# A front of one batch with its divisions split over two engines, its casts moved, its fillers changed and one weight loaded in whole rows

## The chip, the cores and the metric

The kernel runs on one core of one Trainium2 chip. The core has a matrix engine (TensorE, PE in the profile), three engines for elementwise work (VectorE or DVE, ScalarE or ACT, GpSimd or POOL), a queue engine that only issues transfers (SyncE, SP), and 16 DMA engines that all queues share. The metric is the device time of one execution in microseconds, as a median over several runs; lower is better.

## The reference

A linear attention with cosine weights is followed by an MLP mixer. There are 8 batches, 8 heads, 576 positions and 64 channels per head; the result x of the attention has 512 channels.

```python
r = np.maximum(x, 0.0)                       # for q and for k
phi = np.concatenate([r * cos_w, r * sin_w], axis=-1)
kv = np.einsum('bhsf,bhsd->bhfd', k_p, v);  z = np.sum(k_p, axis=2)
num = np.einsum('bhsf,bhfd->bhsd', q_p, kv)
den = np.einsum('bhsf,bhf->bhs', q_p, z)[..., None] + 1e-06
x = num / den                                # heads side by side: (8, 576, 512)
h = np.maximum(xt @ w_tok1, 0.0) @ w_tok2    # xt: x with positions last; 576 -> 256 -> 576
u = x + h.transpose(0, 2, 1)
out = u + np.maximum(u @ w_ch1, 0.0) @ w_ch2 # 512 -> 1536 -> 512
```

Inputs and output are float32; the matmuls of the kernel run in bf16.

## The kernel before

**Tiling.** The 576 positions of a batch are four chunks of 128 (position p * 4 + r is row p of chunk r) and a tail of 64. Tails of two batches share one tile, one in each half of the partitions. The chunks are taken in the order 0, 1, 2, tail, 3 (`ORDER`, line 55).

**Two kinds of work.** A `Front` (lines 217 to 545) makes x and u of a batch: features of q and k (`feature`, line 249), v cast to bf16 (`values`), key sums (`ksum`), the kv matrices (`kv`, `kv_out`), transposes of q's features (`q_trans`), the products `num_half`, the division `x_out` (line 375), the token mixing `tok1` and `tok2`. A `Channel` (lines 550 to 654) makes the two channel matmuls of a batch: `c_main` or `c_block` with w_ch1, ScalarE's ReLU into h1T, `o_step` with w_ch2, and the sum with u and the store.

**What sets the order.** The kernel has a manual schedule: each engine runs its instructions in the order in which the Python code makes them. For batches 1 to 7 a hand-made list (`pieces`, line 473) puts the parts of the next batch's front between the channel steps of the batch before. The first batch has no such cover. Its front is written out in `first_front` (line 656); there TensorE also runs `busy` matmuls (line 203), fillers on zeros that no one reads: 12 at the start, one after each group of q transposes, two for each chunk of k, one and four more later on.

**The end of the first front.** After the kv matrices have been copied out, `cast_tok1` (line 207, ScalarE, twice) casts w_tok1 to bf16. `permute_tok2` (line 210) casts w_tok2 and reorders its columns, one half on ScalarE and one on GpSimd, two instructions each. Then the chunks run in a small pipeline: `num_half` writes one half of the heads (four) into a PSUM tile `num_ps` of two banks, one bank a half; `x_out` multiplies by the reciprocal of the denominator on VectorE, with one instruction for all 8 heads, except that the first chunk goes half by half; `tok1` multiplies the result by w_tok1 into two accumulators. There are two tiles for `num_ps`, so num of a chunk waits until x of the chunk two before has been read out. After the last chunk come `tok1_out` (ReLU into B1), `turned_x` and `turned_b` (u transposed, straight from matmuls), and `c_block` (line 570): for each of the four 128-row blocks of w_ch1 (kb), the first three column blocks of the channel matmul.

**Loads.** SP issues nearly all loads, in program order. At the start come q, k and v of batch 0 in halves, then w_tok1 and w_tok2. w_ch1 is cast to bf16 by its transfer, so GpSimd issues it: four transfers of 128 x 2 x 768, two for the left half of the columns and two for the right (lines 187 to 193); the first waits for the first half of v. `load_batch(1, "kvq")` (line 776) waits for the second of them (`w_ch1_done[1]`), and SP's queue behind it waits too. Later batches' loads stand in the main loop (lines 799 to 811), which for batch 2 loads the tails of both batches of the pair in one go.

Of the kernel before, what the change touches and what calls it, by code (L numbers as in the profile page):

```python
# [9 lines left out]
F32 = mybir.dt.float32  # L10
# [6 lines left out]
def kernel(  # L17
# [15 lines left out]
    nc = tc.nc  # L33
# [149 lines left out]
        nc.gpsimd.memset(t[half(1)], 0.0)  # L183
    for g in range(2):
        nc.gpsimd.dma_start(out=w_tail1[half(g), :], in_=moe_w_tok1[SM:S, :])
    C2 = D_ch // 2
    w_ch1_done = []
    for c2 in range(2):
        for ki in range(0, NCC, 2):
            w_ch1_done.append(nc.gpsimd.dma_start(  # L190
                out=w_ch1[:, ki:ki + 2, c2 * C2:(c2 + 1) * C2],
                in_=moe_w_ch1[ki * P:(ki + 2) * P, c2 * C2:(c2 + 1) * C2]
                .rearrange("(n c) d -> c n d", c=P)))
    after(w_ch1_done[0], v_done)
    w_ch2_done = []
    def load_w_ch2(lo, hi):
# [6 lines left out]
    def busy(dst, times):  # L203
        for _i in range(times):
            nc.tensor.matmul(dst, ident, zeros[:, 0:dst.shape[-1]], start=True, stop=True)

    def cast_tok1(mi):
        nc.scalar.copy(w_tok1[:, :, mi * P:(mi + 1) * P], w_tok1n[:, :, mi * P:(mi + 1) * P])
# [8 lines left out]
    class Front:  # L217
        def __init__(self, b, res, tail):
            self.qt, self.vt, self.kt = io_tiles[b]
            self.va, self.xt = v_augs[b % 2], x_tails[b % 2]  # L220
            self.res, self.tail = res, tail
            self.rows = half(b % 2)

            self.order = ORDER if b != 2 else (*range(R), R)


            self.alone = b < 2
            self.kp, self.qp, self.d_sb = {}, {}, {}

            self.qpT = once.tile([P, R * H, P], BF16, name="qpT")  # L230
            self.kv_sb = [twos.tile([P, HH, DP], BF16, name=f"kv_sb{g}") for g in range(2)]
            self.x = once.tile([P, R, Dm], BF16, name="x_sb")
# [142 lines left out]
        def x_out(self, num_ps, ci, den=None, halves=(0, 2)):  # L375
            lo, hi = halves
            rows = self.rows_of(ci)
            if den is None:
                den = self.d_sb[ci][rows].rearrange("p (g j) o -> p g j o", g=2)
            nv = num_ps[rows, lo:hi, 0:HH * DP].rearrange("p g (j d) -> p g j d", d=DP)  # L380
            nc.vector.tensor_mul(  # L381
                self.x_of(ci)[rows].rearrange("p (g j d) -> p g j d", g=2, j=HH)[:, lo:hi],
                nv[:, :, :, 0:D],
                den[:, lo:hi].to_broadcast([rows.stop - rows.start, hi - lo, HH, D]))

        def tok1(self, mi, chunks):
            if not hasattr(self, "B1"):
# [268 lines left out]
    def first_front(f):  # L656


        idle_ps = ps_at.tile([P, 2, 512], F32, name="idle_ps", tag="at")[:, 0, :]
        lo_heads, hi_heads = (0, HH), (HH, H)  # L660
        busy(idle_ps, 12)

        for j in range(2):
            f.feature("q", 3, j, lo_heads, on_act=True)
        for heads in (lo_heads, hi_heads):
            for ci in range(R):
                if (heads, ci) != (lo_heads, 3):
                    f.feature("q", ci, 0, heads)
                    f.feature("q", ci, 1, heads)
                f.q_trans(ci, heads)  # L670
                busy(idle_ps, 1)
        f.q_side(R)
        f.q_trans(R, pool=ps_at)
        busy(idle_ps, 2)
        for ci in range(R):
            f.feature("k", ci, 0)
            f.feature("k", ci, 1, on_act=(ci > 1))
            busy(idle_ps, 2)
            f.ksum(ci)
        f.k_side(R)  # L680
        f.values(R, nc.vector)
        for ci in range(R):
            f.values(ci, nc.vector, hi_heads)
        for ci in range(R - 1):
            f.values(ci, nc.scalar, lo_heads)
        f.kv(0, (0,))
        busy(idle_ps, 1)
        f.ksum(R)
        f.ksum_out()
        f.values(R - 1, nc.scalar, lo_heads)  # L690
        f.kv(1, (0,))
        f.kv(2, (0,))
        dens = f.dens(ORDER[:2])
        f.dens_out(*dens)
        f.kv(3, (0,))
        f.kv(R, (0,))
        f.kv_out((0,))
        for ci in range(NSC):
            f.kv(ci, (1,))
        f.kv_out((1,), on_act=(1,))  # L700
        for ci in range(NT):
            cast_tok1(ci)
        permute_tok2(0, nc.scalar.copy)
        permute_tok2(1, nc.gpsimd.tensor_copy)
        f.new_uT()
        t_ps = {}

        def num(ci, fill=0):
            num_ps = ps_at.tile([P, 2, 512], F32, name="num_ps", tag="at")
            for g in range(2):  # L710
                f.num_half(num_ps, ci, g)
            busy(num_ps[:, 1, HH * DP:512], fill)
            f.x_out(num_ps, ci)

        num_ps = ps_at.tile([P, 2, 512], F32, name="num_ps", tag="at")
        f.num_half(num_ps, ORDER[0], 0)
        f.x_out(num_ps, ORDER[0], halves=(0, 1))
        dens = f.dens(ORDER[2:])
        f.dens_out(*dens)
        f.num_half(num_ps, ORDER[0], 1)  # L720
        f.x_out(num_ps, ORDER[0], halves=(1, 2))
        num(ORDER[1], fill=4)
        for i, ci in enumerate(ORDER):
            if i + 2 < NSC:
                num(ORDER[i + 2])
            for mi in range(NT):
                f.tok1(mi, (ci,))
            if i == 2:

                for kb in range(2):  # L730
                    t_ps[kb] = ps_mm.tile([P, SM], F32, name="t_ps", tag="mm")
                    f.turned_x(t_ps[kb], kb, ORDER[:2])
        for cols in (slice(0, DH), slice(DH, Dm)):
            for mi in range(NT):
                f.tok1_out(mi, on_act=(mi == 0), cols=cols)
        for kb in range(NCC):
            if kb < 2:
                f.turned_x(t_ps[kb], kb, range(2, R))
                continue
            t_ps[kb] = ps_at.tile([P, 2, 512], F32, name="t_ps", tag="at")[:, 0, :]  # L740
            f.turned_x(t_ps[kb], kb)

        c = Channel(0, f.res, f.tail)
        by_block = f.res["uT"].rearrange("p (r k) t -> p r k t", r=R)
        for kb in range(NCC):
            f.turned_b(t_ps[kb], kb, slice(0, SM))
            (nc.vector.tensor_copy if kb % 2 else nc.scalar.copy)(
                by_block[:, :, kb, :], t_ps[kb].rearrange("p (r t) -> p r t", r=R))
        for kb in range(NCC):
            for mi in range(AHEAD):  # L750
                c.c_block(mi, kb)
        return c

    def load_batch(b, which="kvq", behind=None, main=True, tails=True):
        if b not in io_tiles:
            io_tiles[b] = tiles()
        if b // 2 not in io_tails:
            io_tails[b // 2] = tail_tiles()
        qt, vt, kt = io_tiles[b]
        qtt, vtt, ktt = io_tails[b // 2]  # L760
        done = []
        for n in which:
            dst, tail_dst, src = {"k": (kt, ktt, k), "v": (vt, vtt, v), "q": (qt, qtt, q)}[n]
            if main:
                done.append(load_main(dst, src, b))
            if behind is not None and len(done) == 1:
                after(done[0], behind)
            if tails and b % 2 == 0:
                load_tail(tail_dst, src, b)
            if tails and (b % 2 == 0 or b == 1):  # L770
                load_tail(tail_dst, src, b | 1)
        return done

# [14 lines left out]
    for b in range(B):  # L788
# [4 lines left out]
        for i, step in enumerate(steps):  # L793
            step()
            for what, args in slots.pop(i, ()):
                what(*args)


            if b == 0 and i == NCH:
                load_batch(2, "kq", behind=w_ch2_done[2], tails=False)  # L800
            if b == 0 and i == NCH + 13:
                load_batch(2, "v")
                load_batch(2, "k", main=False)
            if b == 1 and i == 1:
                load_batch(2, "q", main=False)
            if b == 1 and i == 9:
                load_batch(3, "kvq")
            if 1 < b < B - 2 and i == NSC:
                load_batch(b + 2, "vq")
            if 0 < b < B - 3 and i == NCH + 12:  # L810
                load_batch(b + 3, "k")
            if i == len(steps) - 4 and b + 2 < B:
                following = next_front(b + 2)
            for what, args in following.pop(i - len(steps), ()):
                what(*args)
# [34 lines left out]
```

## Time and profile before

| | us |
|---|---|
| median of 3 runs (268.06 to 269.16) | 268.06 |
| the profiled execution, whole | 268.94 |
| its span, first to last instruction | 267.2 |
| TensorE busy in the span | 260.2 (97%) |
| VectorE busy | 165.8 (62%) |
| ScalarE busy | 127.8 (48%) |
| GpSimd busy | 14.1 (5%) |
| first matmul of a filler, first q transpose | 1.37, 6.05 |
| first `c_block` matmul (L574) | 23.58 |

How to read it: a page of the profile gives the busy time of each engine over the span, its share in 40 slices, the DMA queues, the chain of work that ended last, and the costliest groups of instructions. The timeline shows single instructions or merged runs of equal ones: start in us from the span's start, length, engine, source line, operation, output and inputs, the count, and in brackets how long the engine had stood idle just before and what ended that. A busy TensorE isn't TensorE at its peak, since matmuls overlap: a 512-wide bf16 matmul is shown with 0.38 us, while its successor starts 0.22 us after it.

### The profile page before, as it was taken

The numbers are of one execution on the slowest core, as the hardware profiler recorded it, in microseconds if no ns is written. First come the engines' busy times: TensorE is split into PE (matmuls) and PEld (weight loads), VectorE is DVE, ScalarE is ACT, GpSimd is POOL, SyncE is SP. The second block draws the span as 40 slices with busy tenths as digits, with TensorE's granted clock in tenths as the row PEclk, the third lists the DMA queues.
The fourth block names the chain that finished last, engine by engine and source line by source line (L and its number), as shares of the span: only waits on it lengthen the run. The fifth ranks groups of instructions, "written<-read, shape, count | busy, mean of one in ns | idle before, by whom it ended". The sixth has DMA issues, their size and how long they took to land.

```text
span 267.2 us, 5140 instructions
## 1 busy us (share of the span) xinstructions
PE 260.2 (97%) x2042; PEld 139.6 (52%) x2063; DVE 165.8 (62%) x381; ACT 127.8 (48%) x227; POOL 14.1 (5%) x29
## 2 busy tenths in 40 slices
PE   7999999999999999999999999999999999999995
PEld 2575465465644455446644455446644455445544
DVE  6983978785565846876565846876565846720022
ACT  4963794428506462546515362546506362516400
POOL 6060050010000000000000000000000000000000
PEclk9999999999999999999999999999999999999999
DMA  7999999879999999489854999179964570180032
GB/s 219 314 290 259 305 210 205 304 180 288 188 310 306 279 192 324 146 212 262 234 201 118 294 219 349 61 187 237 248 245 118 157 120 0 51 207 1 2 94 102
DMA packets 91079, 53.68 MB, mean 201 GB/s; under 512 B 59440, under 2 KB 85552, under 8 KB 91056
## 3 DMA queue, kind: packets, MB, share of 16 engines
q1 hardware_dynamic: 88288, 49.10, 69.5%
q0 software_dynamic: 2240, 3.74, 7.5%
q10 hardware_dynamic: 528, 0.52, 0.6%
q8 instruction: 16, 0.26, 0.4%
q14 instruction: 7, 0.06, 0.1%
HBM read 35.85 MB, written 9.44 MB: 169 GB/s over the span
## 4 chain that ended last, share of the span: by engine, by line
PE 79%; DMA 9%; DVE 6%; SPq 3%; issue 1%; POOL 0%; ACT 0%
PE o_ps L597 33%; PE c_ps L564 24%; PE u_ps L419 6%; PE b_ps L395 6%; PE ct_ps L584 4%; DMA qt<-in_q_dram 3%; DMA vt<-in_v_dram 3%; DVE x_sb L381 3%; PE kv_ps L324 3%; DMA w_ch<-in_moe_w_ch_dram 3%; SPq L92 2%; PE num_ps L372 2%; SPq L86 1%; DVE den L367 1%; DVE den L366 1%
## 5 line engine op out<-in xcount | busy, mean ns | idle before, releaser
L597 PE MATMUL o_ps<-w_ch,h1T 128*128 128x512 bf16 (+2 forms) x392 | 92.7, 366 | 0.8 <-DMA w_ch<-in_moe_w_ch_dram 0.2
L564 PE MATMUL c_ps<-uT,w_ch 128*128 128x512 bf16 (+2 forms) x384 | 91.5, 372 | 0.0
L568 ACT ACTIVATE h1T<-c_ps 128x512 bf16<-128x512 f32 x93 | 55.3, 598 | 60.0 <-PE c_ps L564 59.8
L597 PEld LDWEIGHTS <-h1T 128*128 128x128 bf16 x408 | 37.6, 98 | 39.7 <-issue 0.5
L564 PEld LDWEIGHTS <-w_ch 128*128 128x128 bf16 x384 | 33.6, 98 | 29.8
L602 DVE TENSOR_TENSOR o_sb<-o_ps,u_sb 128x512 f32<-128x512 f32 (+2 forms) x34 | 22.4, 659 | 29.5 <-PE o_ps L597 29.4
L422 DVE TENSOR_TENSOR u_sb<-u_ps,x_sb 128x512 f32<-128x512 f32 x32 | 21.8, 689 | 8.5 <-PE u_ps L419 6.2
L426 ACT CAST u_bf<-u_sb 128x512 bf16<-128x512 f32 x28 | 17.3, 618 | 16.5 <-DVE u_sb L422 14.8
L419 PE MATMUL u_ps<-B,w_tok 128*128 128x512 bf16 x79 | 22.4, 379 | 0.2
L400 ACT ACTIVATE B<-b_ps 128x512 bf16<-128x512 f32 (+1 forms) x9 | 4.8, 549 | 36.0 <-PE b_ps L395 36.0
L381 DVE TENSOR_TENSOR x_sb<-num_ps,den 128x512 bf16<-128x512 f32 x28 | 19.4, 691 | 1.0
L584 PEld LDWEIGHTS <-w_ch 128*128 128x128 bf16 x192 | 13.9, 98 | 8.7
L395 PE MATMUL b_ps<-x_sb,w_tok 128*128 128x512 bf16 x63 | 17.5, 379 | 0.1
L266 DVE TENSOR_SCALAR qp<-qt,cos_t 128x512 bf16<-128x512 f32 (+1 forms) x35 | 16.2, 463 | 2.1 <-DMA qt<-in_q_dram 2.1
L584 PE MATMUL ct_ps<-uT_tail,w_ch 128*128 128x128 bf16 x192 | 16.9, 219 | 0.0
L277 ACT CAST v_aug<-vt 128x512 bf16<-128x512 f32 (+1 forms) x28 | 15.6, 584 | 0.1
L266 DVE TENSOR_SCALAR kp<-kt,cos_t 128x512 bf16<-128x512 f32 x32 | 15.2, 479 | 0.7 <-DMA kt<-in_k_dram 0.6
L266 DVE TENSOR_SCALAR qp<-qt,sin_t 128x512 bf16<-128x512 f32 (+1 forms) x34 | 15.4, 453 | 0.0
L602 DVE TENSOR_TENSOR o_sb<-o_ps,u_tail 128x512 f32<-128x512 f32 x4 | 2.8, 692 | 19.0 <-PE o_ps L597 19.0
L372 PEld LDWEIGHTS <-qpT 128*128 128x128 bf16 x256 | 11.5, 98 | 4.8 <-issue 0.5
L266 DVE TENSOR_SCALAR kp<-kt,sin_t 128x512 bf16<-128x512 f32 x28 | 13.4, 480 | 0.0
L372 PE MATMUL num_ps<-kv_sb,qpT 128*128 128x65 bf16 x256 | 13.0, 193 | 0.1
(96 smaller groups left out, 223.1 us busy)
## 6 DMA issues: line engine op xcount, KB each, us to landing
out_dram<-o_sb SPq DMA_DIRECT2D x29, 256.0 KB, 2.8
kt<-in_k_dram SPq DMA_DIRECT2D x7, 1024.0 KB, 6.7
vt<-in_v_dram SPq DMA_DIRECT2D x7, 1024.0 KB, 6.4
qt<-in_q_dram SPq DMA_DIRECT2D x7, 1024.0 KB, 8.5
w_ch<-in_moe_w_ch_dram POOLq DMA_DIRECT2D x4, 384.0 KB, 7.8
out_dram<-o_sb SPq DMA_DIRECT2D x9, 128.0 KB, 2.4
qtt<-in_q_dram SPq DMA_DIRECT2D x8, 128.0 KB, 5.3
kt<-in_k_dram SPq DMA_DIRECT2D x2, 512.0 KB, 7.2
```

The source lines that it names most:

```text
L266: nc.vector.tensor_scalar(o_ap, i_ap, scalar1=w, scalar2=0.0, op0=ALU.mult, op1=ALU.max)
L372: nc.tensor.matmul(num_ps[:, g, j * DP:j * DP + D1], self.qT_of(ci, g * HH + j), self.kv_sb[g][:, j, 0:D1], start=True, stop=True)
L381: nc.vector.tensor_mul(self.x_of(ci)[rows].rearrange("p (g j d) -> p g j d", g=2, j=HH)[:, lo:hi], nv[:, :, :, 0:D], den[:, lo:hi].to_broa ...
L395: nc.tensor.matmul(self.b1_ps[mi], w, self.x_of(ci), start=(ci == self.order[0]), stop=(ci == self.order[-1]))
L419: nc.tensor.matmul(u_ps, w_tok2[:, ki, ci * P:(ci + 1) * P], self.B1[:, ki, :], start=(ki == 0), stop=(ki == NT - 1))
L422: nc.vector.tensor_add(u, u_ps[rows], self.x_of(ci)[rows])
L426: nc.scalar.copy(self.ub[:, ci, :], u)
L564: nc.tensor.matmul(c_ps[:, lo:hi], w_ch1_of[:, ki, mi // 2, mi % 2, :], uT[:, lo // P:hi // P, ki, :], start=(ki == 0), stop=(ki == NCC - 1))
L568: nc.scalar.activation(self.h1T[:, mi, :], c_ps, AF.Relu)
L584: nc.tensor.matmul(self.ct_ps[:, mi % R, :], w_ch1_of[:, ki, mi // 2, mi % 2, :], self.tail.uT[:, ki, :], start=(mi % R == 0 and ki == 0), ...
L597: nc.tensor.matmul(o_ps, h, w_ch2[:, ki, cols], start=ki == 0, stop=ki == NCH - 1)
L602: nc.vector.tensor_add(o_sb, o_ps, u)
```

## The change

- w_ch1 is loaded in four transfers of 128 whole rows of 1536 instead of four of 2 x 128 half rows. `w_ch1_done[1]` is then the second block of rows.
- A new filler, `busy_long`, multiplies 256 float32 columns of the same zeros by 128 float32 columns of them. Five of it stand for the 12 fillers at the start, one for each pair (one of the pairs is that behind the q transposes of the tail). The single fillers and the four in `num` stay.
- In the first batch VectorE divides three heads of each half (`n = HH - 1`), and ScalarE the fourth, one activation per half with the reciprocal as its scale: two per chunk.
- Both halves of w_tok2 are permuted by GpSimd.
- `cast_tok1(0)` and `cast_tok1(1)` move behind the first and the second half of the first chunk's x.
- The load of v's tail of batch 3 moves from `load_batch(2, "v")`, in batch 0's steps, to behind the load of q's tails in batch 1's second step.

```diff
-    C2 = D_ch // 2
     w_ch1_done = []
-    for c2 in range(2):
-        for ki in range(0, NCC, 2):
-            w_ch1_done.append(nc.gpsimd.dma_start(
-                out=w_ch1[:, ki:ki + 2, c2 * C2:(c2 + 1) * C2],
-                in_=moe_w_ch1[ki * P:(ki + 2) * P, c2 * C2:(c2 + 1) * C2]
-                .rearrange("(n c) d -> c n d", c=P)))
+    for ki in range(NCC):
+        w_ch1_done.append(nc.gpsimd.dma_start(out=w_ch1[:, ki, :],
+                                              in_=moe_w_ch1[ki * P:(ki + 1) * P, :]))
...
+    zeros32 = zeros.bitcast(F32)
+
+    def busy_long(dst, times):
+        for _i in range(times):
+            nc.tensor.matmul(dst[:, 0:256], zeros32[:, 0:P], zeros32, start=True, stop=True)
...
+            self.first = b == 0
...
-            nc.vector.tensor_mul(
-                self.x_of(ci)[rows].rearrange("p (g j d) -> p g j d", g=2, j=HH)[:, lo:hi],
-                nv[:, :, :, 0:D],
-                den[:, lo:hi].to_broadcast([rows.stop - rows.start, hi - lo, HH, D]))
+            x = self.x_of(ci)[rows].rearrange("p (g j d) -> p g j d", g=2, j=HH)
+            n = HH - 1 if self.first else HH
+            nc.vector.tensor_mul(
+                x[:, lo:hi, 0:n], nv[:, :, 0:n, 0:D],
+                den[:, lo:hi, 0:n].to_broadcast([rows.stop - rows.start, hi - lo, n, D]))
+            for j in range(n, HH):
+                for g in range(lo, hi):
+                    nc.scalar.activation(x[:, g, j], nv[:, g - lo, j, 0:D], AF.Copy,
+                                         scale=den[:, g, j])
...
-        busy(idle_ps, 12)
+        busy_long(idle_ps, 5)
...
         f.q_trans(R, pool=ps_at)
-        busy(idle_ps, 2)
+        busy_long(idle_ps, 1)
         for ci in range(R):
             f.feature("k", ci, 0)
             f.feature("k", ci, 1, on_act=(ci > 1))
-            busy(idle_ps, 2)
+            busy_long(idle_ps, 1)
             f.ksum(ci)
...
         f.kv_out((1,), on_act=(1,))
-        for ci in range(NT):
-            cast_tok1(ci)
-        permute_tok2(0, nc.scalar.copy)
+        permute_tok2(0, nc.gpsimd.tensor_copy)
         permute_tok2(1, nc.gpsimd.tensor_copy)
...
         f.x_out(num_ps, ORDER[0], halves=(0, 1))
+        cast_tok1(0)
         dens = f.dens(ORDER[2:])
         f.dens_out(*dens)
         f.num_half(num_ps, ORDER[0], 1)
         f.x_out(num_ps, ORDER[0], halves=(1, 2))
+        cast_tok1(1)
         num(ORDER[1], fill=4)
...
-            if tails and (b % 2 == 0 or b == 1):
+            if tails and odd and (b % 2 == 0 or b == 1):
                 load_tail(tail_dst, src, b | 1)
...
             if b == 0 and i == NCH + 13:
-                load_batch(2, "v")
+                load_batch(2, "v", odd=False)
                 load_batch(2, "k", main=False)
             if b == 1 and i == 1:
                 load_batch(2, "q", main=False)
+                load_tail(io_tails[1][1], v, 3)
```

More of the change, by code (lines that the diff above doesn't have):

```diff
@@ L752, in first_front, with load_batch @@
         return c
-    def load_batch(b, which="kvq", behind=None, main=True, tails=True):
+    def load_batch(b, which="kvq", behind=None, main=True, tails=True, odd=True):
         if b not in io_tiles:
```

## The prediction

> **What bounds the kernel now.** I read the page first. TensorE (PE) is busy 97% of the span, and the granted clock is full in every slice; so outside a few waits the time is the length of PE's list of matmuls, and an edit can gain only where PE waits or where filler matmuls run. All edits lie in the first batch's front or in the loads. Second, therefore, the timeline of the front:
>
> ```profile
> 17.88 0.40 PE L372 MATMUL num_ps<-kv_sb,qpT 128*128 128x65 bf16 x8
> 18.33 0.38 PE L395 MATMUL b_ps<-x_sb,w_tok 128*128 128x512 bf16 x1
> 18.58 0.57 PE L372 MATMUL num_ps<-kv_sb,qpT_tail 128*128 128x65 bf16 x8
> 18.99 0.59 PE L395 MATMUL b_ps<-x_sb,w_tok 128*128 128x512 bf16 x2
> 19.42 0.41 PE L372 MATMUL num_ps<-kv_sb,qpT 128*128 128x65 bf16 x8
> ...
> 20.32 0.59 PE L395 MATMUL b_ps<-x_tail,w_tail 128*128 128x512 bf16 x2
> 20.75 0.59 PE L395 MATMUL b_ps<-x_sb,w_tok 128*128 128x512 bf16 x2
> ```
> ```profile
> 16.45 0.42 DVE L381 TENSOR_TENSOR x_sb<-num_ps,d_sb 128x256 bf16<-128x256 f32 x1 [0.25 <-PE num_ps L372]
> ...
> 19.19 0.68 DVE L381 TENSOR_TENSOR x_tail<-num_ps,d_sb 64x512 bf16<-64x512 f32 x1
> 19.87 0.69 DVE L381 TENSOR_TENSOR x_sb<-num_ps,d_sb 128x512 bf16<-128x512 f32 x1
> ```
> ```profile
> 5.37 0.60 ACT L264 ACTIVATE qp<-qt,bias,cos_t 128x256 bf16<-128x256 f32 x1 [1.96 <-DMA qt<-in_q_dram]
> ...
> 14.51 0.41 ACT L277 CAST v_aug<-vt 128x256 bf16<-128x256 f32 x1
> ...
> 16.60 1.14 ACT L208 CAST w_tok<-u_sb 128x512 bf16<-128x512 f32 x2
> ```
>
> The columns are start, length, engine, line, operation. VectorE (DVE) is filled from 16.45 to 20.56 by the divisions (L381) and the two small steps before them, which looks like the bound. It is not: after 17.88 PE has no wait in this view. The last x chunk ends at 19.87 + 0.69 = 20.56 and PE takes it at 20.75, when its own list has come there. From 18 to 36 us PE is dense, so whatever makes it later here is passed on. ScalarE's rows are for the prices below.
>
> Third, PE's waits behind that stretch, and the chain that ended last:
>
> ```profile
> 37.76 0.62 PE L344 MATMUL qT_ps<-ident,qp 128*128 128x128 bf16 x8 [0.28 <-DVE qp L266]
> 38.55 0.62 PE L344 MATMUL qT_ps<-ident,qp 128*128 128x128 bf16 x8 [0.17 <-DVE qp L266]
> ...
> 43.17 1.02 PE L597 MATMUL o_ps<-w_ch,h1T 128*128 128x512 bf16 x3 [0.20 <-DMA w_ch<-in_moe_w_ch_dram]
> ```
> ```profile
> 14.26 7.21 DMA w_ch<-in_moe_w_ch_dram
> ...
> 27.40 9.11 DMA qt<-in_q_dram
> ```
>
> The second batch's loads start when the second w_ch1 transfer lands (14.26 + 7.21 = 21.47), and q, the last of them, ends the wait at 37.76. That chain costs PE only 0.28 + 0.17 + 0.20 = 0.65 us: a buffer which takes up lateness from the front.
>
> **The change, part by part.**
>
> *x split between VectorE and ScalarE.* Each 512-wide division becomes 384 wide on VectorE plus two 64-wide activations on ScalarE. VectorE's price per element is (0.69 - 0.42) / 256 = 1.05 ns, so 128 fewer save 0.13 us each. ScalarE's price for 64 elements has no row. 128x256 takes 0.41 us without pointer operands and 0.60 with two (scale and bias), so about 0.50 with one; 192 elements fewer, at (0.80 - 0.60) / 256 = 0.8 ns (128x512 with two pointers: 0.80), take off 0.16: 0.34 us. The ends are 0.17 (the 128x8 cast at L296) and 0.50. Followers start 0.10 early (5.37 + 0.60 against 5.87), so a pair takes 0.34 + 0.24 = 0.58.
>
> The waits decide. In the changed program's order each ScalarE piece waits for VectorE's product of the same chunk, although it needs none of it: the split puts the pieces behind one another. And what waited for the product now waits for the pieces: the second half of the first chunk's num (PE waits for the first piece), each num that takes the buffer, the matmuls of tok1. On ScalarE cast_tok1(0) stands between the first two pieces, cast_tok1(1) before the second chunk's. With 0.06 us from an end to a waiting start (16.87 to 16.93):
> - first piece: VectorE ends at 16.45 + 0.35 = 16.80, piece 16.86 to 17.20, num's second half at 17.26 instead of 16.93.
> - VectorE's second product then starts at 17.60 instead of 17.46, ends at 17.89; piece 17.95 to 18.29; third num at 18.35 instead of 17.88.
> - cast_tok1(1) runs 18.19 to 18.81, so the second tok1 is at 18.87 instead of 18.33.
> - chunk 1: num and its four fillers end 0.33 later, VectorE 18.17 to 18.73, pieces to 19.37, num of the tail at 19.43 instead of 18.58 (+0.85).
> - tail: VectorE 20.04 to 20.60, pieces to 21.24, tok1 at 21.30 instead of 20.32 (+0.98).
> - last chunk: num at 20.27, VectorE 20.73 to 21.29, pieces to 21.93, tok1 at 21.99 instead of 20.75: **+1.24 us**.
>
> With ScalarE at 0.17 the same steps give about +0.7, with 0.50 about +1.8. Below nothing only if the waits were shorter than ordered; that is a rival.
>
> Here the trace shows no two engines reading one PSUM tile together. [...]
>
> *Both permutations of w_tok2 on GpSimd.* Four casts instead of two: GpSimd's first pair starts at 17.39 and takes 1.11 + 0.30, so both end at 17.39 + 2 x 1.41 = 20.2 us. Their reader (L445) starts at 21.85, so 1.6 us of PE's tok1 work covers them; that cover grows with the lateness above. ScalarE's 1.43 us for them goes, which makes room for the pieces; it was off the path. If each took twice as long, they would end at 23.0: +1.2 on the old schedule, none on the late one. I take nothing.
>
> *w_ch1 in whole rows.* The same bytes in four transfers, half the pieces. An issue on GpSimd of 256 pieces takes 0.74 us, of 128 (L605) 0.61: some 0.13 earlier each. How long a row takes to move has no row here; between nothing gained and a transfer's whole spacing: landings run from 13.1 + 6.5 = 19.6 to 15.7 + 9.5 = 25.2, or 1.87 each. I take 0.15 each, as the issue is the nearest row; the gate then opens about 0.4 early, and q too. Since PE arrives at 37.48 + 1.24, no one waits for q and this gain is worth nothing. On the other side, PE now needs all four transfers by its tenth block matmul: 23.58 + 9 x 0.217 = 25.5 (where before the first two sufficed), 26.8 with the lateness; the last landed at 25.2. Cost nothing; 1.6 us of cover.
>
> *Fillers.* Twelve 512-wide bf16 matmuls become five 256-wide f32 ones, pairs become one. No f32 matmul is in the trace. If each takes the time of two bf16 ones, five end at 1.15 + 5 x 0.84 = 5.4 us (early ones stand 0.42 apart: three take 1.46, the last of them 0.63), before the first transposes at 6.05, and a pair's successor costs the same 0.43 (later ones stand 0.217 apart: four take 1.03, the last 0.38). I take this: zero. The bounds are a quarter of it (bf16 speed) and double; both are the slower rival.
>
> *One load moved* (v's tail of batch 3, 0.65 us of SP's queue, from before the k tails to behind the q tails): the second to fourth transposes of q in that queue have the same work ahead of them as before, the first has 0.65 less, and PE shows no wait there. Zero; 0.3 either way.
>
> **Sum.** +1.24 in the front, of which 0.65 is taken up at 37 to 43 us: **+0.6**; with the bounds of ScalarE's price +0.05 to +1.15. The profiled execution took 268.94 us (span 267.2, 1.7 around it); the median is 268.06. From the profiled time: 269.5; from the median, **268.6**, which I give.
>
> **Rivals.**
> - *The split relieves.* For it: VectorE is full for 4.1 us and loses 6 x 0.13 at most. Against: PE, not VectorE, is dense there. The front stays, and the earlier q removes up to 0.45 of the wait: 267.6. Chance 0.20.
> - *The new fillers don't stand in for the old* (slower). [...] Above (6.05 - 1.15) / 5 = 0.98 us each they hold up the transposes and ScalarE's full row of copies behind them: at 1.28 us, 1.5 us later, less the 0.51 us by which VectorE waits for v at 14.6, so +1.0 on top of +0.6: 269.7; at double, +3. [...] Against: the sizes match. Chance 0.15. [...]
> - *w_ch1 comes late.* If whole rows took over 0.4 us more each, the fourth lands after 26.8 and the block matmuls wait; at double the spacing it lands 4 x 1.87 later, 32.7, +6; at half as much again, 28.9, +2.1 on top: 270.7. Against: same bytes, longer pieces. Chance 0.03.
> - If rows don't come earlier at all, w_ch1's edit does nothing and the forecast stands.
>
> **Numbers.** Forecast 0.62 (own range 267.9 to 269.3), relief 0.20, fillers 0.15, w_ch1 0.03. The range that leaves out two in ten is 267.4 to 269.8: the forecast's bounds, most of the relief, and the mild end of the fillers. 0.5%, about what a measurement of this kernel can tell from no change, is 1.34 us: 266.7 to 269.4. Slower: 0.62 x 0.1 + 0.15 x 0.8 + 0.03 = 0.21; faster: 0.03, from the relief with a front that also gains; within: 0.76.
>
> **What would show it.** Pieces of x on ScalarE that begin after VectorE's product of the same chunk; the tail's num near 19.4, the last tok1 near 22.0, the block matmuls near 24.8 instead of 23.58; no wait at the transposes near 38. A front that starts its blocks by 23.6 makes the first step wrong; transposes that start after 6.1, or early matmuls of 0.63 us beyond 6 us, point to the fillers; a wait of L574 for w_ch1 to the third rival.

## The result and the profile after

| | before | after |
|---|---|---|
| median, us (21 runs each) | 268.06 (267.62 to 269.16) | 268.92 (268.72 to 270.95) |
| the profiled execution, its span | 268.94, 267.2 | 268.82, 266.9 |
| first block matmul (L574, after: L583) | 23.58 | 24.39 |
| waits of PE from 35 to 45 us (those in brackets) | 0.65 | none |

The ratio of after to before is 1.0037, with an interval of 1.0026 to 1.0049: slower by 0.86 us. That is less than the 0.5% named in the prediction, but the whole interval lies above 1, so the loss is real.

The page of the changed kernel, busy times and the shares of the chain that ended last:

```profile
PE 260.8 (98%) x2061; PEld 142.2 (53%) x2061; DVE 164.9 (62%) x381; ACT 129.1 (48%) x235; POOL 14.8 (6%) x31
...
PE 94%; DVE 3%; DMA 2%; ACT 0%; issue 0%; DVEq 0%
```

DMA is 2% of the chain (9% in the first profile of before, 13% in a second one): in this execution batch 1's transfers hardly decide any more. TensorE's timeline there, in the changed kernel:

```profile
17.22 0.52 PE L376 MATMUL num_ps<-kv_sb,qpT 128*128 128x65 bf16 x12 [0.22 <-ACT x_sb L392]
...
18.36 0.40 PE L376 MATMUL num_ps<-kv_sb,qpT 128*128 128x65 bf16 x8 [0.29 <-ACT x_sb L392]
18.60 0.66 PE L404 MATMUL b_ps<-x_sb,w_tok 128*128 128x512 bf16 x2
19.29 0.40 PE L376 MATMUL num_ps<-kv_sb,qpT_tail 128*128 128x65 bf16 x8
...
21.56 0.59 PE L404 MATMUL b_ps<-x_sb,w_tok 128*128 128x512 bf16 x2
```

The brackets name the new releaser: num waits for ScalarE's pieces (`<-ACT x_sb`), where these rows had no bracket before. The first of them writes the other bank of `num_ps` than the piece reads, and waits all the same. ScalarE's timeline in the changed kernel shows what the pieces wait for:

```profile
16.85 0.31 ACT L392 ACTIVATE x_sb<-num_ps,d_sb 128x64 bf16<-128x64 f32 x1 [0.15 <-DVE x_sb L387]
...
18.00 0.31 ACT L392 ACTIVATE x_sb<-num_ps,d_sb 128x64 bf16<-128x64 f32 x1 [0.33 <-DVE x_sb L387]
...
18.72 0.52 ACT L392 ACTIVATE x_sb<-num_ps,d_sb 128x64 bf16<-128x64 f32 x2
...
20.31 0.51 ACT L392 ACTIVATE x_tail<-num_ps,d_sb 64x64 bf16<-64x64 f32 x2 [0.40 <-DVE x_tail L387]
```

ScalarE stood idle until VectorE's product of the same chunk released it (`<-DVE x_sb`, `x_tail`); of the six rows of pieces only the pair at 18.72 has no bracket, since it came behind a cast on its own engine. And VectorE, which in the shown rows of before ran without a gap from 19.19, has gaps now:

```profile
19.73 0.55 DVE L387 TENSOR_TENSOR x_tail<-num_ps,d_sb 64x384 bf16<-64x384 f32 x1 [0.37 <-PE num_ps L376]
```

The division is 0.13 us shorter, as priced (0.55 against 0.68), and VectorE waits 0.37 us for a num that itself waited for ScalarE. Behind the blocks, in the changed kernel, the transposes near 38 us stand without a wait:

```profile
38.13 1.06 PE L348 MATMUL qT_ps<-ident,qp 128*128 128x128 bf16 x16
```

### The profile page after: what moved, and what is told of

It is laid out like the page before. It is cut to its first block, busy times and chain, and to the rows that moved or that the text cites. A ratio compares the mean times of both kernels' runs of the same rounds, so it can differ in the third digit from the quotient of the medians.

```text
span 266.9 us, 5165 instructions
## 1 busy us (share of the span) xinstructions
PE 260.8 (98%) x2061; PEld 142.2 (53%) x2061; DVE 164.9 (62%) x381; ACT 129.1 (48%) x235; POOL 14.8 (6%) x31
## 4 chain that ended last, share of the span: by engine, by line
PE 94%; DVE 3%; DMA 2%; ACT 0%; issue 0%; DVEq 0%
PE o_ps L606 35%; PE c_ps L573 30%; PE u_ps L428 7%; PE b_ps L404 6%; PE ct_ps L593 4%; PE kv_ps L328 4%; PE num_ps L376 4%; DMA qt<-in_q_dram 2%; DVE qp L270 1%; PE qT_ps L348 1%; PE c_ps L583 1%; PE idle_ps L207 1%; PE t_ps L454 1%; PE d_ps L308 0%; DVE x_sb L387 0%; PE ks_ps L292 0%
## 5 line engine op out<-in xcount | busy, mean ns | idle before, releaser
L606 PE MATMUL o_ps<-w_ch,h1T 128*128 128x512 bf16 (+2 forms) x408 | 94.2, 366 | 0.0
```

Of the source, the lines that this page charges most:

```text
L606: nc.tensor.matmul(o_ps, h, w_ch2[:, ki, cols], start=ki == 0, stop=ki == NCH - 1)
```

## The experiments

The theory (A in the expectations) is the prediction's: what ScalarE's pieces add to the chain of num, product, piece and next num is the loss, and the time of any version is the start of its first block plus the late waits plus a constant. One rival puts the loss into another part of the change, the fillers above all; another puts it behind the front. Each kernel was run twelve times (the one with both casts ahead: six times) beside the kernel before on the same chip, whose median was 268.11 us for the first four kernels and 268.00 for the last four.

**The kernel before once more** (before_again), since its first profiled execution lies 0.9 us over its median.

> The kernel before, once more, for a second profile. Theory A (the first profile of before, 268.94 us, was one of its long executions, and its 0.65 us of waits for q, k and w_ch2 at 37 to 43 us belong to that length): a profile near 268.0 with those waits under 0.2 us and v's first half landed by about 12.3 us instead of 12.8, and block matmuls still near 23.3 to 23.6. Rival B (the waits are always there, and the time differs elsewhere): a profile near 268.0 with the same 0.65 us of waits. Median 268.06 either way.

Median 267.96 us, ratio 0.9991 (0.9974 to 1.0007); the profiled execution took 268.33. TensorE's timeline in this second profile of before:

```profile
18.65 0.39 PE L372 MATMUL num_ps<-kv_sb,qpT_tail 128*128 128x65 bf16 x7 [0.20 <-issue]
...
23.46 0.81 PE L574 MATMUL c_ps<-uT,w_ch 128*128 128x512 bf16 x3
...
42.57 1.02 PE L597 MATMUL o_ps<-w_ch,h1T 128*128 128x512 bf16 x3 [0.35 <-DMA w_ch<-in_moe_w_ch_dram]
```

v's first half landed at 12.40 us instead of 12.79. The waits at the transposes are gone; the one for w_ch2 is larger than expected, 0.35. So neither theory held whole, and the 0.65 us buffer of the prediction isn't a fixed property of the kernel. And PE pauses for 0.20 us inside the tail's num with nothing to wait for (`<-issue`). The same pause is in the first profile: there the tail's num took 0.57 us, where eight such matmuls otherwise take 0.40.

**The change without the split.** (no_split)

```diff
-            self.first = b == 0
+            self.first = False
```

> The changed kernel with x divided by VectorE alone again; casts, GpSimd's permutations, fillers, w_ch1 rows and the moved load stay as changed. Theory A (the serial wait for ScalarE's pieces is the loss of 0.86 us): 268.1 to 268.3, the block matmuls 0.7 to 0.9 us earlier than the changed kernel's 24.39. Rival B (the new fillers, 0.25 us a pass against 0.22, and the later first transposes are half of it or more): 268.5 or more. Rival C (moving the casts behind the halves holds up the first tok1): second tok1 still near 18.9 and 268.5 or more.

Median 267.98 us, ratio 0.9985 (0.9966 to 1.0003). TensorE's timeline in it, for the rows that wait in the changed kernel:

```profile
17.87 0.40 PE L376 MATMUL num_ps<-kv_sb,qpT 128*128 128x65 bf16 x8
...
18.57 0.40 PE L376 MATMUL num_ps<-kv_sb,qpT_tail 128*128 128x65 bf16 x8
...
20.57 0.59 PE L404 MATMUL b_ps<-x_sb,w_tok 128*128 128x512 bf16 x2
...
23.40 0.81 PE L583 MATMUL c_ps<-uT,w_ch 128*128 128x512 bf16 x3
```

No row has a bracket. All other parts of the change are in, and the block starts 0.99 us earlier than in the changed kernel (23.40 against 24.39, a little more than expected); the median is 0.94 lower. Together the other parts leave at most 0.08 us of loss over the kernel before (the interval's upper end), so the rival that puts the loss into another part falls.

**The split alone** (split_alone): the kernel before with the split, and the casts and permutations moved that make room for it on ScalarE; fillers and w_ch1 as before.

```diff
-        for ci in range(NT):
-            cast_tok1(ci)
-        permute_tok2(0, nc.scalar.copy)
+        permute_tok2(0, nc.gpsimd.tensor_copy)
...
+        cast_tok1(0)
...
+        cast_tok1(1)
```

(`x_out` as in the change.)

> The kernel before with the division split, the casts moved and both permutations on GpSimd; old fillers, w_ch1 in half rows, the load where it was. Theory A: the whole loss, 268.8 to 269.0, or a little less if the new fillers cost 0.1 to 0.2. Rival B (fillers): 268.3 or less.

Median 269.03 us, ratio 1.0027 (1.0009 to 1.0046). TensorE's timeline in it:

```profile
16.82 0.52 PE L380 MATMUL num_ps<-kv_sb,qpT 128*128 128x65 bf16 x12 [0.22 <-ACT x_sb L396]
...
17.96 0.40 PE L380 MATMUL num_ps<-kv_sb,qpT 128*128 128x65 bf16 x8 [0.29 <-ACT x_sb L396]
...
23.99 0.38 PE L587 MATMUL c_ps<-uT,w_ch 128*128 128x512 bf16 x1
```

The same two waits, 0.22 and 0.29, as in the changed kernel. The split brings the loss by itself; the casts and permutations that come with it here stand in the version without the split too, where nothing is lost.

**The split with its order of waits undone.** (own_tile) ScalarE's heads (6 and 7 instead of 3 and 7) go into a PSUM tile of their own, so that a piece waits for the matmuls and the reciprocal only; to make room, the transposes of the first two chunks' x move behind the last tok1.

```diff
+            if self.first:
+                if g == 1:
+                    self.act_ps = ps_mm.tile([P, 2, DP], F32, name="act_ps", tag="mm")
...
+                for h in (H - 2, H - 1):
+                    nc.scalar.activation(x[:, h], self.act_ps[rows, h - H + 2, 0:D], AF.Copy,
+                                         scale=den[:, h])
```

> The changed kernel with ScalarE's two heads (the last two, 6 and 7) written to a PSUM tile of their own, so that its pieces wait for the matmuls and the reciprocal only, not for VectorE's product, and the second half of the first num no longer waits for a piece; the first two turned chunks move behind the last tok1 to free the banks, with the same matmuls. Theory A (the serial waits, not ScalarE's work, are the loss): 267.9 to 268.3, the second half of the first num near 16.8, the third num near 17.9. Rival D (ScalarE's work in the path is itself the loss, pieces of 0.3 us behind casts of 0.6): 268.6 or more, with PE waiting for ScalarE's x at the same places.

Median 268.04 us, ratio 1.0001 (0.9980 to 1.0021). ScalarE's timeline in it, and then VectorE's:

```profile
18.11 0.94 ACT L409 ACTIVATE x_sb<-act_ps,d_sb 128x64 bf16<-128x64 f32 x4
19.17 0.51 ACT L409 ACTIVATE x_tail<-act_ps,d_sb 64x64 bf16<-64x64 f32 x2
19.85 0.52 ACT L409 ACTIVATE x_sb<-act_ps,d_sb 128x64 bf16<-128x64 f32 x2 [0.17 <-PE act_ps L381]
```
```profile
17.39 1.39 DVE L404 TENSOR_TENSOR x_sb<-num_ps,d_sb 128x128 bf16<-128x128 f32 x3
...
19.79 0.56 DVE L404 TENSOR_TENSOR x_sb<-num_ps,d_sb 128x384 bf16<-128x384 f32 x1
```

No bracket names VectorE on ScalarE's side any more: the four pieces at 18.11 start while VectorE's products run (17.39 to 18.78), and the last pair begins at 19.85, beside VectorE's product (19.79 to 20.35) and not behind it. The block starts at 23.56 instead of 24.39, with the same work on both engines. So it was the order, not ScalarE's price, that cost the time. Both engines still write one tile of x, so that was not what ordered them. The edit takes away both orders at once (a piece behind the product, the next num behind a piece) and gives ScalarE another bank as well as another tile of PSUM; what each is worth was not told apart. Over the version without the split (23.40) nothing is gained. From the first num to the third it takes 1.62 us (16.05 to 17.67) instead of 1.75 (16.12 to 17.87), so VectorE had held PE up by 0.13; behind that PE loses as much again, since w_tok1's second cast (17.60 to 18.22) now stands behind two pieces on ScalarE. The rest of the difference is a pause of some 0.2 us in this execution (further below).

**w_ch1 in whole rows, alone.** (w_ch1_alone)

```diff
-    for c2 in range(2):
-        for ki in range(0, NCC, 2):
...
+    for ki in range(NCC):
+        w_ch1_done.append(nc.gpsimd.dma_start(out=w_ch1[:, ki, :],
+                                              in_=moe_w_ch1[ki * P:(ki + 1) * P, :]))
```

> The kernel before with one part of the change, w_ch1 in whole rows. Theory A (the profiled time is the start of the first channel block, plus the waits of TensorE between 35 and 45 us, plus about 244.5; whole rows take those waits away): block near 23.5 as in the kernel before, no wait of over 0.1 us on PE between 35 and 45, profiled time 267.9 to 268.1, ratio near 0.999. Rival B (the waits went with another part, the permutations or the moved load): the wait for w_ch2 of 0.25 to 0.35 us near 42.6 stays and the time is that of before, 268.1 to 268.4.

Median 268.12 us, ratio 1.0004 (0.9987 to 1.0021). Its profiled execution was its shortest, 267.46; TensorE's timeline in it:

```profile
11.66 0.59 PE L201 MATMUL idle_ps<-zeros,ident 128*128 128x512 bf16 x2
12.09 0.34 PE L284 MATMUL ks_ps<-ones,kp 128*128 128x1 bf16 x8
...
23.05 1.24 PE L570 MATMUL c_ps<-uT,w_ch 128*128 128x512 bf16 x5
```

No wait from 35 to 45 us, as theory A wanted of the profile, but the median is that of before. The block at 23.05 shows before's front without its pauses: from the third num (17.51 here, 17.56 in the second profile of before) to the block it takes 5.54 us here and 5.90 there, so that the pauses are worth 0.36.

**The new fillers, alone.** (fillers_alone)

```diff
-        busy(idle_ps, 12)
+        busy_long(idle_ps, 5)
...
-            busy(idle_ps, 2)
+            busy_long(idle_ps, 1)
```

> The kernel before with one part of the change, the float32 fillers. Theory A: each filler pair ends about 0.07 us later than two bf16 fillers while the clock is full, so the first channel block starts 0.1 to 0.3 us later than in the kernel before (23.55 to 23.75 beside 23.46), the wait for w_ch2 shrinks by as much, and the median stays within 0.2 us of before (ratio 1.000). Rival B (the float32 fillers do not keep the clock up): PE's granted clock in the first 20 us is lower than in the kernel before, the block starts over 0.5 us later, and the median is 0.4 us or more above.

Median 268.30 us, ratio 1.0007 (0.9991 to 1.0023). TensorE's timeline in it:

```profile
6.51 0.63 PE L205 MATMUL idle_ps<-zeros,ident 128*128 128x512 bf16 x1
...
11.72 0.68 PE L211 MATMUL idle_ps<-zeros 128*128 128x256 f32 x2
12.25 0.35 PE L294 MATMUL ks_ps<-ones,kp 128*128 128x1 bf16 x8
...
23.38 1.89 PE L580 MATMUL c_ps<-uT,w_ch 128*128 128x512 bf16 x8
...
37.93 0.62 PE L350 MATMUL qT_ps<-ident,qp 128*128 128x128 bf16 x8 [0.65 <-DVE qp L272]
```

One f32 filler is shown as two records (the x2 is one filler). Its successor starts 0.53 us after it here, where two bf16 fillers took 12.09 - 11.66 = 0.43. That puts the block at 23.38, 0.33 us behind w_ch1_alone's 23.05: a little over theory A's 0.1 to 0.3, against a front without pauses; against the second profile of before (23.46), for which theory A was given, the block is not later. The median is 0.3 us above before's, but the ratio's interval (-0.24 to +0.62 us) leaves open whether that is a loss. Rival B's signs are absent: the granted clock is shown full (1.00) over the first 20 us (0.999 over the whole execution) and the block is not 0.5 us later. Theory A wanted the late wait to shrink; the waits came to 0.82 us, all at the transposes.

**Both casts of w_tok1 ahead of the pieces again.** (casts_ahead)

```diff
+        for ci in range(NT):
+            cast_tok1(ci)
         permute_tok2(0, nc.gpsimd.tensor_copy)
...
-        cast_tok1(0)
...
-        cast_tok1(1)
```

> The changed kernel with both casts of w_tok1 put back ahead of the first chunk's x, as in the kernel before; ScalarE's pieces stay. Theory A (ScalarE's pieces are in series with VectorE's product and each is waited for by the next num): the first piece begins near 17.6 instead of 16.85, since 1.1 to 1.2 us of casts stand ahead of it, and num's second half, tok1 and the block start 0.3 to 0.8 us later than in the changed kernel: block 24.7 to 25.2, median 269.2 to 269.7. Rival B (the casts would run in ScalarE's idle time before the product and hide): the first piece at 16.85 to 17.0, block at 24.4 or earlier, median 268.6 to 268.9.

Median 270.25 us, ratio 1.0069 (1.0047 to 1.0092). ScalarE's timeline in it, then TensorE's:

```profile
17.67 0.32 ACT L392 ACTIVATE x_sb<-num_ps,d_sb 128x64 bf16<-128x64 f32 x1
```
```profile
18.04 0.53 PE L376 MATMUL num_ps<-kv_sb,qpT 128*128 128x65 bf16 x12 [0.99 <-ACT x_sb L392]
...
25.21 0.59 PE L583 MATMUL c_ps<-uT,w_ch 128*128 128x512 bf16 x2
```

The first piece comes 0.82 us later (17.67 against 16.85), num waits 0.99 instead of 0.22, and the block starts 0.82 later: a delay of a piece is passed on whole. The median is 0.55 above the expected top. Of the profiled 270.10 - 268.82 = 1.28, 0.33 is a wait for w_ch2 at 44.31, which the expectation had not. Whole rows did not take it away, nor did a front that is later than any other.

**The best of both: the tile of its own, with the old fillers.** (own_old_fill) The edit is that of the fillers, undone in own_tile.

> The kernel own_tile (ScalarE's heads in a PSUM tile of their own) with the bf16 fillers of the kernel before. Theory A: the float32 fillers held up the chain by 0.1 to 0.3 us, so the block starts at 23.25 to 23.5 instead of 23.56, no wait at 35 to 45 us, median 267.7 to 268.0, ratio 0.998 to 1.000. Rival B (the chain there is set by VectorE and ScalarE, not by fillers): block at 23.56 and the median of own_tile, 268.0 to 268.1.

The profiled execution took 267.89 us, its block starts at 23.09 (own_tile: 23.56), no wait from 35 to 45. But the median is 268.48, above both expectations, ratio 1.0006 (0.9992 to 1.0020). Of the 0.47 by which the block comes earlier, some 0.2 is a pause in own_tile's tail num (0.58 us there for six matmuls, otherwise 0.34); the rest goes with the fillers. No version beat the kernel before beyond its interval.

All ten profiles, in us, with the sum that theory A makes (the waits are those that the timeline of PE shows with a bracket):

| kernel | profiled time | block start | waits 35 to 45 | the rest |
|---|---|---|---|---|
| w_ch1_alone | 267.46 | 23.05 | 0 | 244.41 |
| no_split | 267.72 | 23.40 | 0 | 244.32 |
| own_old_fill | 267.89 | 23.09 | 0 | 244.80 |
| own_tile | 268.05 | 23.56 | 0 | 244.49 |
| before, second | 268.33 | 23.46 | 0.35 | 244.52 |
| split_alone | 268.81 | 23.99 | 0.25 | 244.57 |
| after | 268.82 | 24.39 | 0 | 244.43 |
| before, first | 268.94 | 23.58 | 0.65 | 244.71 |
| fillers_alone | 268.99 | 23.38 | 0.82 | 244.79 |
| casts_ahead | 270.10 | 25.21 | 0.33 | 244.56 |

The rest stays within 0.5 us while the times differ by 2.6: nothing behind 45 us depends on the change by more than that. The rival that puts the loss behind the front falls.

The sum is an account and not a cause where a wait stands: there block start and wait together give the time at which a load landed. In casts_ahead the chain that ended last runs until 44.3 us through loads and what issues them (v of batch 0, w_ch1, v of batch 1, w_ch2), not through the front, and in split_alone likewise until 43.0. How early this chain is differs from one execution to the next: w_ch1's first issue stands at 12.29 us in the changed kernel's profile, at 13.08 in the first of before, and between 12.56 and 12.78 in the other eight. So that the changed kernel's profile has no late wait is in part a matter of which execution was profiled.

## Why the prediction was right, point by point

**The mechanism.** "In the changed program's order each ScalarE piece waits for VectorE's product of the same chunk, although it needs none of it": shown by the pieces' releasers, by no_split (the loss goes with the split) and by own_tile (it goes with the order, at the same work). ScalarE's piece takes 0.31 us (0.34 on record). The first steps met their times: first piece 16.85 (16.86 on record), num's second half 17.22 (17.26), second piece 18.00 (17.95), third num 18.36 (18.35), second tok1 18.88 (18.87), which is the end of the row of two matmuls, 18.60 + 0.66, less the 0.38 of one.

That they meet on the clock is luck in part. VectorE's first product starts at 16.45 us before and at 16.46 after, although the new fillers, put at nothing, cost time ahead of it: before's profiled front lost about as much by a pause in its kv matmuls (16 of them in 0.85 us, 0.65 in the changed kernel) and by a key sum that came 0.58 us behind the start of its fillers (0.43 in w_ch1_alone). In w_ch1_alone, with neither, the first num stands at 15.77 us instead of 16.12 and 16.14.

**The size of +1.24 was wrong.** From the step "num of the tail at 19.43" on, the steps come later than the trace: 19.29 there, last tok1 at 21.56 instead of 21.99. Two terms were mis-sized. The pair of pieces was put at 0.58 us and takes 0.52; it stands twice on the way to the last tok1, 0.12 in all. And the tail's num went in with the 0.57 us of before's row; 0.17 of that is PE's pause, which the changed kernel does not have (0.40), and it made both "VectorE 20.04" and "num at 20.27" late. A row's length was taken for the price of its work. The other 0.14 of the 0.43 lies in starts that came sooner than 0.06 us behind an end (the last pair at 20.99, its product's end at 20.96). Against no_split the delay is +0.99; against the first profile of before it is 24.39 - 23.58 = +0.81, since that profile held pauses and a later start of its own.

**"A buffer which takes up lateness from the front", 0.65 us.** In that one execution the account closes: 0.81 more in the front, 0.65 less in the waits, and 268.82 against 268.94 with 0.28 of the rest's spread. But the step "from the median, 268.6" carried the buffer over to executions in which it is smaller (0.35 in the second profile), and in which it need not move with the front (casts_ahead). The medians differ by 0.86 and the front's shift is 0.81 to 0.99, so between the medians at most 0.13 us was taken up. Two errors lay against each other, by luck: 0.25 to 0.43 too much in the front, 0.5 to 0.7 too much in the buffer. The forecast of 268.6 was 0.3 us below the 268.92 measured.

**Permutations on GpSimd, at nothing.** They ran from 16.46 to 19.11 us, before their reader at 22.66; no_split, which has them, shows no loss.

**w_ch1 in whole rows, worth nothing.** Right for the median (1.0004). In the profiles, five of six kernels with whole rows have no wait from 35 to 45 us, and all four with half rows have 0.25 to 0.82. A median without a gain does not settle whether that is a small effect or the draw, but the step through which it was to come is not there: from the first issue of w_ch1 to SP's first load of batch 1 it takes 8.18 to 8.89 us (mean 8.45) with whole rows and 8.35 to 8.86 (mean 8.52) with half rows, not the 0.4 less on record. The rival "w_ch1 comes late" did not occur. TensorE's weight loads (PEld) for the block wait for w_ch1 for up to 0.25 us at some 25.3 us in one kernel with whole rows (own_tile) and two with half rows, but the twelve matmuls lose nothing: 2.75 us there, as in no_split.

**Fillers, "zero".** One f32 filler of 256 columns takes the time of two bf16 ones of 512, as assumed, and some 0.1 us on top (0.53 us to its successor against 0.43). Over the front that makes some 0.33 us (fillers_alone 23.38, w_ch1_alone 23.05), which the prediction put at nothing. The five at the start ended at 1.20 + 4.24 = 5.44 (5.4 on record), in the other kernels with them between 5.21 and 5.84. The rival "don't stand in" did not occur. PE's first transpose stands at 6.19 in the changed kernel, past the 6.1 named as a sign, but PE had stood idle for 0.76 us until VectorE's features came, and the next matmuls have their later lengths (0.38 us for 512 columns at 6.42). No run has fillers of a quarter of the assumed time, so nothing shows that they would make the kernel slower, as the prediction counts its lower bound.

**"The split relieves"** fell: own_tile is the nearest to a relief that was run, and its block comes no earlier than no_split's (23.56 against 23.40). ScalarE and VectorE read different banks of PSUM side by side there: the last pair of pieces took 0.52 us beside a product of 0.56 us, the lengths that they had one after the other in the changed kernel (0.52 at 20.99, 0.56 at 20.40). Two engines on one bank were not tried.

**The load moved, zero**: no wait at batch 1's transposes in the changed kernel. Alone it was not tried.

## What to carry to other kernels

Before a step is split over two engines, ask whom the next step waits for, and whether the program lets the two halves run side by side: where they share a tile (or a bank of it, which was not told apart here), the second half may be queued behind the first, and the shorter instruction makes the chain longer (here VectorE's division became 0.13 us shorter and the block came 0.99 us later than without the split). Price a chain from rows without a pause (eight matmuls at 0.40, not the one row at 0.57). And a buffer seen in one execution belongs to that execution: look at a second profile before it is carried over to the median, and ask which chain ends the wait.

## What was not expected of the hardware

- TensorE pauses by 0.2 to 0.4 us in the tail's num in three of the ten profiles (both of before, own_tile) and not in the other seven. In the second profile of before nothing is shown to wait for (`<-issue`). No run shows the cause.
- In fillers_alone the matmuls kept their early length (0.63 us for 512 columns) until about 7 us, in the changed kernel, with the same fillers at the start, the first such matmul behind them (at 6.42) took 0.38. The block's start did not suffer: 23.38.
- Executions of one kernel spread over 1.7 to 2.5 us (267.43 to 269.14 in 29 runs of before, 267.60 to 270.07 in 35 others), more than any part of the change is worth, so parts of 0.3 us show in a profile's rows and not in a median of 12 runs.
